# Moving two weight splits between engines and one step earlier, and two small TensorE steps one place later, in a fused attention and expert kernel

## The chip, the core and the metric

The kernel runs on one core of one Trainium2 chip. The metric is the device time of one execution in microseconds (us). PE is the matrix engine, PEld its weight loads, DVE the vector engine, ACT the scalar engine, POOL the GpSimd engine, SP the engine that issues most of the transfers (DMAs).

## The reference

The first half is attention with a window. For each of 4 batches and 8 heads, 768 rows of 64 numbers attend to the 31 rows around them and to 24 summaries, one for each block of 32 rows (the maximum of the keys, the mean of the values):

```python
scores_l = scale * np.matmul(q, k.transpose(0, 1, 3, 2))
scores_s = scale * np.einsum('bhsd,bhnd->bhsn', q, k_sum) + np.log(block)
a = softmax(concat(where(mask_l, scores_l, -1e9), scores_s))
out = a @ concat(v, v_sum)
```

The second half takes the 4 x 768 rows of 512 numbers (x), computes 8 gate logits and one more logit for each row, and picks one of 8 experts: the row's own best one where it is the first of its batch or its extra logit is negative, and otherwise the expert of the row before it. The row goes through that expert (`relu(x @ w1[e]) @ w2[e]`) and is scaled by the softmax weight of the expert.

## The kernel before

**Attention.** There are 16 pairs of heads (4 batches of 4 pairs), and each pair is done in two steps of 384 rows: 32 steps, G = 0 to 31, in `attention()`. Step G issues, in this order: the scores of step G (`s_mm`, L264 and L270), the transposes of the probabilities of step G-2 (`t_stage`, L291, copied by ACT in L292), the row maximum on DVE (L277) and six exponentials on ACT (L281) of step G, then the product with the values of step G-3 (`a_mm`, L302) and its division on DVE (`a_norm`, L313 to L315). Even steps prepare keys for a later pair on POOL (`windows`, L228), take a maximum over keys on DVE (L202) and fold the values on POOL (L213); odd steps write the summaries of keys (L231) and of values (`spread_v`, L242) on POOL. All engines work through their instructions in the order of issue. The scores of an even step G = 2n read the keys that L228 and L231 wrote for pair n.

Two score buffers alternate. From G = 32 on there are no more scores: the memory of the score buffers is given to other uses (`free_banks`), and the first `a_mm` after it writes into what was the buffer of step 31.

**The gate, beside attention.** Each of the 24 tiles of 128 rows goes through `x_tile`: (1) four transposes (L477) and a copy by ACT (L486); (2) products with the gate weights, in four quarters (L495); (3) a copy by ACT (L498); (4) a product that sums the four quarters (L506); (5) a copy by DVE to `l_all` (L508). For the first three batches the five parts are hung on steps of attention (`XT`, and the list in L1173). For the last batch they stand in `last()`, which runs 16 times `next(first)`, one eighth of a matmul stage of the first pair of expert blocks (six matmuls of 128 x 256), and after each does the parts of the gate tiles that are due: tile u starts at k = `XA[u]`, and its five parts come at k - `XA[u]` in `XL`. From G = 32 on each gate tile uses two of a pool of three PSUM banks, one for its transposes and one for parts 2 to 5.

**The routing** of a batch (`route`) is a chain of some 30 tiny DVE instructions and four PE steps (L539, L545, L551, L572), which follow one another. Such chains are generators that yield the kind of the next step ("DVE", "PE", "LONG", ...). During attention `small(n)` is called three times in each step G (with 3, 2 and 4 credits, the first after the exponentials are issued, the second before `a_norm`, the third at the end): it issues up to n steps of the first two chains in the list, a "PE" step only if two calls have passed since the chain's last step and a "PE late" step only if three have (`ON_PE`, L57). From G = 32 on `flow()` does the same by modelled times. The chain of batch 0 starts in G = 15 and picks the expert whose weights are fetched first (`have_e0`), that of batch 1 in G = 23; after it follow the index lists for the first blocks (`early`, `index`, whose L778 releases two gathers on POOL, L1001) and the gate's softmax (`gate_p`: a DVE subtraction L682, an exponential on ACT L683, and DVE sums from L687 on).

**The first expert's weights.** The fp32 weights are used as two parts, a rounded high part and a low part. Eight chunks of 128 x 1024 (j = 0 to 3 of `w1`, 4 to 7 of `w2`) are fetched by SP at the steps G in `WFETCH`; chunk j is split at step `WSPLIT[j]` for j < 4 (and at k in `WLAST` for j = 4 to 7). `split` casts on ACT (L987), then subtracts, on DVE as one instruction (L990) or on POOL as four (L995), as `WBY[j]` says ("V" or "G"). The splits stand at the end of a step, after `a_norm`.

**The experts.** Then follow pairs of blocks of 128 gathered rows (`pair`): 4 x 4 parts of six matmuls each for the first product (L1056 to L1058), relu on ACT (L1062), low part on DVE (L1064), and 16 parts for the second (L1029 to L1031). `tx` transposes gathered rows (L1012) and splits them (L1005 on ACT, L1007 on DVE).

Of the kernel before, what the change touches and what calls it, by code (L numbers as in the profile page):

```python
# [38 lines left out]
WARM = 44  # L39

WFETCH = (21, 21, 22, 22, 26, 27, 31, 32)
WSPLIT = (24, 25, 30, 31)
WBY = "VGGVVGVG"

WLAST = (2, 5, 8, 11)
XT = (0, 0, 1, 2, 2, 3)

START = ((33, 1), (34, 0), (34, 1))
XA = (0, 2, 4, 6, 8, 10)
XL = (0, 2, 3, 4, 5)  # L50

SPLIT_BY = ("VGVV", "VGVG")

# [10 lines left out]
class Kernel:  # L64
# [446 lines left out]
    def route(self, b):  # L511
# [28 lines left out]
        pm = wk.tile([NU, P], F32, name="pm")  # L540
        yield "DVE"
        v.tensor_tensor_scan(out=pm, data0=m[0:NU, 0:P], data1=self.zero[0:NU, 0:P], initial=0.0, op0=ALU.max, op1=ALU.max)
        yield "PE"
        m = self.bank("t")
        nc.tensor.transpose(out=m[:, 0:NU], in_=pm, identity=self.ident[0:NU, 0:NU])  # L545
        vm = wk.tile([P, NU], F32, name="vm")
# [569 lines left out]
    def run(self):  # L1116
# [5 lines left out]
        def at(G, point, f, *args):  # L1122
            jobs.setdefault((G, point), []).append((f, args))

        def tiles(f, b, k):
            if (b, k) not in st:
                st[b, k] = f(b, k)
            next(st[b, k], None)
# [6 lines left out]
        def wsplit(j):  # L1135
            w, q = divmod(j, NCH)
            self.split(w, q * CH, (q + 1) * CH, st.pop(("w", j)), nc.vector if WBY[j] == "V" else nc.gpsimd)

        def have_e0():
            st["e0"] = nc.values_load(self.e0[0:1, 0:1], engines=(ENG.SP,), min_val=0, max_val=E - 1)  # L1140
            for j in range(2 * NCH):
                if j < NCH:
                    at(WSPLIT[j], 1, wsplit, j)
                at(WFETCH[j], 1, wfetch, j)
# [44 lines left out]
        def last():  # L1189
            for k in range(XA[-1] + XL[-1] + 1):  # L1190
                next(first)
                if k in WLAST:
                    wsplit(NCH + WLAST.index(k))
                for u in range(NU):
                    if k - XA[u] in XL:
                        tiles(self.x_tile, B - 1, u)
                self.flow(C_T)
            self.later(self.wait(), self.route(B - 1), self.finish())
# [186 lines left out]
```

## Time and profile before

| what | value |
|---|---|
| three runs | 473.49, 472.39, 473.93 us; median 473.49 |
| the profiled execution | 473.66 us, of which the span of instructions is 471.8 |
| PE busy | 440.5 us, 93% of the span |
| DVE, ACT, POOL busy | 254.9, 216.5, 225.2 us |
| mean granted clock of PE | 0.976 |
| attention, first to last score product | to about 122.6 us |
| first matmul of the first pair of blocks | 133.80 us |

A row of the timeline reads: start, duration (of all merged instructions), engine, line, operation, what it writes <- what it reads, sizes, count, and in brackets how long its engine stood idle before it and what ended that. A row of the waits reads: who waited on whom, total us, how often, the longest. A row of the windows reads: the stretch and its length, then for PE, PEld, DVE, ACT and POOL the busy time and in parentheses the instructions begun, then the granted PE clock, the busy share of the DMA engines and GB/s.

### The profile page before, as it was taken

The page shows a single profiled execution, that of the slowest core. Times are in us where ns is not written, and L with a number is a line of the kernel's source. Part 1 is how long each engine was busy: PE and PEld are TensorE (multiplying, and loading weights), DVE is VectorE, ACT ScalarE, POOL GpSimd, SP SyncE. Part 2 cuts the span into 40 slices and gives each one's busy share as a digit, 9 for nine tenths or more (in the row PEclk, how much of TensorE's full clock was granted, in tenths as well). Part 3 has the DMA queues.
Part 4 walks back from the last instruction along what each step waited for, and adds up shares of the span by engine and source line. Part 5 has one row for each costly group of instructions (what it writes and reads, how often), then busy time and mean ns, then how long its engine had stood idle before and what let it go on. Part 6 is the DMA issues. An engine that isn't in the chain of part 4 may idle for free. (4 is left out here: it accounts for less than half of the span.)

```text
span 471.8 us, 12078 instructions
## 1 busy us (share of the span) xinstructions
PE 440.5 (93%) x4400; PEld 383.6 (81%) x4400; DVE 254.9 (54%) x603; ACT 216.5 (46%) x480; POOL 225.2 (48%) x316
## 2 busy tenths in 40 slices
PE   7799989979799999999999999999999999999990
PEld 6687767767687789798989898989779898978970
DVE  4776697868764788981222222363654227274510
ACT  4888887778745124612202020263673027266410
POOL 2686676675502421932030303094987207588820
PEclk9999999979999999999999999999999999999996
DMA  8999879988250390472020202047489403938840
GB/s 316 374 384 384 345 254 393 377 299 303 83 188 2 106 383 13 160 277 69 24 68 24 67 24 69 22 158 291 146 304 338 154 23 102 345 115 319 302 172 26
DMA packets 23623, 92.05 MB, mean 195 GB/s; under 512 B 2927, under 2 KB 3567, under 8 KB 19440
## 3 DMA queue, kind: packets, MB, share of 16 engines
q1 hardware_dynamic: 18752, 76.11, 43.6%
q0 software_dynamic: 4640, 14.68, 9.4%
q8 instruction: 41, 0.67, 0.6%
q14 instruction: 46, 0.38, 0.3%
q10 hardware_dynamic: 144, 0.20, 0.1%
HBM read 78.40 MB, written 13.11 MB: 194 GB/s over the span
## 5 line engine op out<-in xcount | busy, mean ns | idle before, releaser
L1058 PE MATMUL bs<-xT,l 128*128 128x256 f32 x384 | 108.9, 284 | 1.4 <-DVE l L990 1.4
L1056 PE MATMUL bs<-xT,h 128*128 128x256 f32 x384 | 109.9, 286 | 0.0
L1057 PE MATMUL bs<-xT,h 128*128 128x256 f32 x384 | 108.8, 283 | 0.5 <-DVE xT L1007 0.5
L1001 POOL DMA_INDIRECT xg<-x_dram,gidx x32 | 37.1, 1160 | 122.2 <-PE bt L1012 53.2
L1062 ACT ACTIVATE hT<-bs 128x512 fp32r<-128x512 f32 x48 | 28.7, 598 | 121.9 <-PE bs L1058 121.4
L1064 DVE SCALAR_TENSOR_TENSOR hT<-bs,hT 128x512 fp32r<-128x512 f32 x48 | 33.1, 690 | 90.6 <-ACT hT L1062 79.7
L1029 PE MATMUL ba<-h,hT 128*128 128x512 f32 x192 | 77.8, 405 | 0.5
L995 POOL TENSOR_TENSOR l<-stg,h 128x256 fp32r<-128x256 f32 x84 | 74.6, 921 | 2.5 <-ACT h L987 1.6
L1058 PEld LDWEIGHTS bs<-xT,l 128*128 128x128 f32 x384 | 73.5, 191 | 2.0 <-DVE l L990 2.0
L1031 PE MATMUL ba<-h,hT 128*128 128x512 f32 x192 | 75.1, 391 | 0.0
L1030 PE MATMUL ba<-l,hT 128*128 128x512 f32 x192 | 75.1, 391 | 0.0
L1057 PEld LDWEIGHTS bs<-xT,h 128*128 128x128 f32 x384 | 73.5, 192 | 1.4 <-DVE xT L1007 1.0
L1056 PEld LDWEIGHTS bs<-xT,h 128*128 128x128 f32 x384 | 73.5, 191 | 0.7 <-issue 0.2
L987 ACT CAST h<-stg 128x1024 fp32r<-128x1024 f32 x56 | 57.3, 1052 | 12.2 <-PE ba L1031 10.9
L281 ACT ACTIVATE pr<-bs,nm 128x120 f32<-128x120 f32 x192 | 51.6, 367 | 13.0 <-DVE nm L277 12.8
L990 DVE TENSOR_TENSOR l<-stg,h 128x1024 fp32r<-128x1024 f32 x35 | 47.4, 1364 | 16.3 <-ACT h L987 13.1
L1042 POOL DMA_INDIRECT out_dram<-yo,sidx x26 | 28.0, 1076 | 46.4 <-DVE yo L1041 21.3
L1029 PEld LDWEIGHTS ba<-h,hT 128*128 128x128 f32 x192 | 36.1, 188 | 8.1 <-ACT h L987 0.5
L1031 PEld LDWEIGHTS ba<-h,hT 128*128 128x128 f32 x192 | 36.0, 188 | 7.9
L1030 PEld LDWEIGHTS ba<-l,hT 128*128 128x128 f32 x192 | 36.2, 189 | 6.2
L242 POOL COPY vw<-vs 24x384 f32<-24x384 f32 x64 | 30.7, 521 | 8.7 <-ACT vs L237 6.1
L302 PE MATMUL ba<-vw,pt 120*64 120x65 f32 x768 | 31.5, 235 | 2.9 <-POOL vw L242 2.4
(236 smaller groups left out, 663.4 us busy)
## 6 DMA issues: line engine op xcount, KB each, us to landing
stg<-in_w SPq DMA_DIRECT2D x32, 1024.0 KB, 6.9
vw<-in_vW SPq DMA_DIRECT2D x16, 780.0 KB, 7.6
kp<-in_kT SPq DMA_DIRECT2D x16, 384.0 KB, 6.9
q<-in_qT SPq DMA_DIRECT2D x16, 384.0 KB, 7.4
vt<-in_vT SPq DMA_DIRECT2D x16, 384.0 KB, 8.1
x_dram<-xs SPq DMA_DIRECT2D x8, 768.0 KB, 5.1
wst<-in_w SPq DMA_DIRECT2D x8, 512.0 KB, 6.7
xg<-x_dram,gidx POOLq DMA_INDIRECT x32, 3.9
```

Source lines behind the costliest of these rows:

```text
L281: nc.scalar.activation(out=pr[:, h, u, :], in_=sp[:, h, u, :], func=AF.Exp, bias=nm[:, h, u:u + 1], scale=1.0)
L987: self.nc.scalar.copy(out=hi, in_=src)
L990: eng.tensor_tensor(out=lo, in0=src, in1=hi.bitcast(F32), op=ALU.subtract)
L995: eng.tensor_tensor(out=lo[:, p], in0=src[:, p], in1=hi[:, p].bitcast(F32), op=ALU.subtract)
L1001: self.nc.gpsimd.indirect_dma_start(out=t, out_offset=None, in_=rows, in_offset=bass.IndirectOffsetOnAxis(ap=self.gidx[:, i:i + 1], axis=0))
L1029: nc.tensor.matmul(out=ps, lhsT=ah, rhs=wh, start=first, stop=False)
L1030: nc.tensor.matmul(out=ps, lhsT=ah, rhs=wl, start=False, stop=False)
L1031: nc.tensor.matmul(out=ps, lhsT=al, rhs=wh, start=False, stop=last)
L1056: nc.tensor.matmul(out=ps[:, j], lhsT=wh, rhs=xh, start=(k == 0), stop=False)
L1057: nc.tensor.matmul(out=ps[:, j], lhsT=wh, rhs=xl, start=False, stop=False)
L1058: nc.tensor.matmul(out=ps[:, j], lhsT=wl, rhs=xh, start=False, stop=(k == KT - 1))
L1064: nc.vector.scalar_tensor_tensor(out=l, in0=ps, scalar=0.0, in1=h.bitcast(F32), op0=ALU.max, op1=ALU.subtract)
```

## The change

Four edits:

1. Chunk 0 is split in G = 23 in place of G = 24, on POOL in place of DVE.
2. Chunk 2 (G = 30) is split on DVE in place of POOL, chunk 3 (G = 31) on POOL in place of DVE.
3. In `last()` parts 4 and 5 of each gate tile come one k later, so the loop takes 17 turns in place of 16.
4. The second PE step of the routing (L545) waits for three calls of `small` in place of two, for batches 0 and 1.

```diff
 WFETCH = (21, 21, 22, 22, 26, 27, 31, 32)
-WSPLIT = (24, 25, 30, 31)
-WBY = "VGGVVGVG"
+WSPLIT = (23, 25, 30, 31)
+WBY = "GGVGVGVG"
...
-XL = (0, 2, 3, 4, 5)
+XL = (0, 2, 3, 5, 6)
...
         v.tensor_tensor_scan(out=pm, data0=m[0:NU, 0:P], data1=self.zero[0:NU, 0:P], initial=0.0, op0=ALU.max, op1=ALU.max)
-        yield "PE"
+        yield "PE late" if b < 2 else "PE"
         m = self.bank("t")
         nc.tensor.transpose(out=m[:, 0:NU], in_=pm, identity=self.ident[0:NU, 0:NU])
```

## The prediction

> **What bounds the kernel now.** I read the page first, then PE's waits, then the windows around PE's long gaps, then the timelines of each engine there.
>
> ```profile
> span 471.8 us, 12078 instructions
> ...
> PE   7799989979799999999999999999999999999990
> ```
>
> PE is the bound, and after slice 14 (11.8 us each) it is full until the last one. So what PE loses or gains before about 160 us reaches the end undiminished, and the change lies there.
>
> ```profile
> 65.46 0.19 PE L545 MATMUL bt<-ident,pm 6*128 6x6 f32 x1 [0.96 <-DVE pm L542]
> 98.20 0.24 PE L545 MATMUL bt<-ident,pm 6*128 6x6 f32 x1 [3.13 <-DVE pm L542]
> 127.90 1.48 PE L302 MATMUL ba<-vw,pt 120*64 120x65 f32 x24 [2.38 <-POOL vw L242]
> 134.72 0.39 PE L1057 MATMUL bs<-xT,h 128*128 128x256 f32 x1 [0.54 <-DVE xT L1007]
> 144.50 0.39 PE L506 MATMUL bt<-c,l 128*128 128x9 f32 x2 [0.42 <-ACT l L498]
> 153.69 0.39 PE L506 MATMUL bt<-c,l 128*128 128x9 f32 x2 [0.90 <-ACT l L498]
> ```
>
> These waits of PE between 60 and 160 us are what the edits touch: 0.96 and 3.13 (edit 4, the second with edit 1), 2.38 (edit 2), 0.42 and 0.90 (edit 3). Two of them cost more than their length:
>
> ```profile
> 93.90:97.32 3.42, 0.97 (x25) 0.81 (x24) 2.61 (x3) 2.39 (x6) 2.42 (x4) 1.00 1.05 422
> 97.40:100.70 3.30, 2.50 (x33) 2.14 (x34) 1.99 (x7) 2.76 (x8) 1.02 (x3) 0.50 0.40 155
> 100.80:104.10 3.30, 3.30 (x35) 3.15 (x34) 1.64 (x5) 2.47 (x8) 3.30 (x6) 0.50 1.00 304
> 124.63:128.04 3.41, 1.03 (x10) 0.65 (x12) 3.27 (x12) 2.53 (x9) 3.34 (x6) 1.00 0.00 0
> 128.10:131.40 3.30, 3.30 (x42) 2.84 (x41) 2.68 (x9) 2.35 (x5) 1.11 (x3) 0.50 0.58 176
> ```
>
> Where PE was busy 0.97 or 1.03 us of 3.4, the next 3.4 us ran at a granted clock of 0.50, and after a stretch with 2.50 of 3.30 one more did. A half-speed stretch that sets the end costs half of 3.4, 1.7 us. I call it a cold window. [...]
>
> **A. Edit 4, batch 0.** L545 moves from the last call of G = 17 to the first of G = 18, behind the next scores and transposes. Its input is ready then, so the 0.96 goes: between -1.0 and 0 (if DVE or ACT holds PE back by as much a step later). I take -0.9: the wait's own row is the nearest. Each later step of the chain also moves one call, `have_e0` from the end of G = 20 to the start of G = 21, still ahead of the fetches there, so SP's order stays.
>
> **B. Edits 1 and 4, batch 1 (G = 23 to 26).**
>
> ```profile
> 94.45 1.08 ACT L987 CAST h<-wst 128x1024 fp32r<-128x1024 f32 x1
> 95.56 1.35 DVE L990 TENSOR_TENSOR l<-wst,h 128x1024 fp32r<-128x1024 f32 x1 [0.81 <-ACT h L987]
> 96.83 0.90 DVE L277 TENSOR_REDUCE nm<-bs 128x6 f32<-128x720 f32 x1
> 92.98 1.62 ACT L281 ACTIVATE pr<-bs,nm 128x120 f32<-128x120 f32 x6 [1.17 <-DVE nm L277]
> 90.66 1.46 POOL L228 TENSOR_SCALAR kb<-kp 128x384 f32<-128x384 f32 x3
> 92.08 1.15 POOL L213 TENSOR_TENSOR vf<-vt 128x192 f32<-128x192 f32 x2
> 94.84 0.43 POOL L231 TENSOR_SCALAR kb<-ks 128x288 f32<-128x288 f32 x1 [1.61 <-DVE ks L202]
> 100.45 2.77 POOL L995 TENSOR_TENSOR l<-wst,h 128x256 fp32r<-128x256 f32 x4 [2.28 <-issue]
> 98.67 1.41 PE L270 MATMUL bs<-kb,q 64*64 64x120 f32 x24
> ```
>
> The 3.13 us come from DVE, which waits 0.81 for the cast of chunk 0, splits it (1.35), and only then reaches L277 and the scan. Both leave DVE. The cast fits into the 1.17 that ACT idles one step earlier. But POOL now does 2.77 us between the summaries of pair 11 and the keys of pair 13. POOL was free at 90.66; the cast ends at about 91.6 there, the split at 91.7 + 2.8 = 94.5, L228 at 96.0, L213 at 97.1, L231 at 97.6. The scores of G = 26 read what L231 writes, so PE, which would be there at 95.1, waits until 97.7; they began at 98.67 before, behind L545 and the mask products. So POOL takes DVE's place as the releaser, and the start moves by -0.8 (0 to -1.0). The gap of 2.5 us still leaves a window with about 1 us of work, so one cold window stays; the second, which followed 2.50 of 3.30 busy, may go: up to -1.7, and -2.9 (half of the 2.50 + 3.30 done cold) if both go; 0 if neither. PE is not alone in setting the pace there, so I take -1.0. B: -1.8.
>
> **C. Edit 2 and the shifted chain (G = 30 to 34).**
>
> ```profile
> 118.95 0.15 DVE L774 COPY tl<-bt 128x2 f32<-128x2 f32 x1
> 120.89 0.90 DVE L277 TENSOR_REDUCE nm<-bs 128x6 f32<-128x720 f32 x1
> 123.30 1.08 ACT L987 CAST h<-wst 128x1024 fp32r<-128x1024 f32 x1
> 124.59 0.25 DVE L687 TENSOR_REDUCE sm<-ex 128x12 f32<-128x96 f32 x1 [1.03 <-ACT ex L683]
> 126.19 1.62 ACT L281 ACTIVATE pr<-bs,nm 128x120 f32<-128x120 f32 x6 [0.88 <-DVE nm L277]
> 128.77 1.52 DVE L990 TENSOR_TENSOR l<-wst,h 128x1024 fp32r<-128x1024 f32 x1 [0.55 <-ACT h L987]
> 133.39 1.28 DVE L1007 TENSOR_TENSOR xT<-bt,xT 128x512 fp32r<-128x512 f32 x2
> ```
>
> The wait at 127.90 is booked to POOL's L242, but that copy belongs to pair 15 and the product is of pair 14. It writes into the score buffer of step 31, whose last exponential ends at 126.19 + 1.62 = 127.81, and PE starts 0.09 later. So freeing POOL does not help it, and a DVE split ahead of L277 of step 31 hurts it. From then on DVE runs nearly without a pause up to L1007, which releases PE's L1057. So I count DVE from L277 of step 30 (120.89) to the end of L1007 (134.67), 13.8 us with pauses of 1.03 and 0.55. After the change: L774 to L778 fall behind that L277, +0.6; the split is done beside an idle POOL, -0.2; DVE waits for the cast of chunk 2 (after its division at 123.4 until 124.4), 1.0; and L683 is now issued behind the exponentials of step 31, so that DVE waits from the end of L682 to the end of L281 plus one ACTIVATE, 1.65. Pauses 2.65 against 1.58: +1.1. The scores of step 30 come 0.4 earlier, as L732 moves behind them. Sum: 0.6 - 0.2 + 1.1 - 0.4 = +1.1, and +0.1 for small DVE work beside POOL's split: +1.2 (from -0.5, if DVE catches up in the time that its missing split leaves, to +2).
>
> **D. Edit 3, and three banks.**
>
> ```profile
> 142.00 0.66 PE L477 MATMUL bt<-ident,xs 128*128 128x128 f32 x4
> 142.41 0.36 PE L1056 MATMUL bs<-xT,h 128*128 128x256 f32 x1
> 148.22 0.66 PE L477 MATMUL bt<-ident,xs 128*128 128x128 f32 x4
> 142.75 0.59 ACT L486 COPY hs<-bt 128x512 f32<-128x512 f32 x1 [1.52 <-PE bt L477]
> 148.56 1.23 DVE L990 TENSOR_TENSOR l<-wst,h 128x1024 fp32r<-128x1024 f32 x1
> 149.70 0.16 DVE L508 COPY l_all<-bt 128x9 f32<-128x9 f32 x1
> ```
>
> L506 one k later finds its copy done: -0.42 - 0.90 = -1.3. But a tile now keeps its bank until k + 6 in place of k + 5, and the next tiles start every second k, so at each even k two tiles hold banks and everything else shares the third. Two places: at k = 8 the transposes of tile 4 (148.22) need the bank that L508 of tile 1 frees, and L508 stands behind the DVE split of chunk 6, so at 149.86: +1.6. At k = 4 the routing's L551 (one step later, since the DVE work modelled before it grew) needs the bank that L486 frees at 142.75 + 0.59 = 143.34, and PE would go on at 142.41: +0.9. Sum +1.2 (-1.3 if another bank is free in both, +1.6 if more waits follow). The last batch's routing starts one k later; it runs under matmuls: 0, and 0.7 at most, the length of a k.
>
> **E. Cold windows.** PE's gaps in C and D grow: it waits some 3 us for step 31, then some 2 for L1007, and 1.6 in D. Of 3.4 us that is the share of the rows above that were followed by clock 0.50, and behind L1057 PE alone sets the pace. I take one cold window more: +1.7 (0 to +3.4).
>
> **Sum**: -0.9 - 1.8 + 1.2 + 1.2 + 1.7 = +1.4 on the profiled execution's 473.66 (span 471.8 and 1.9 around it), 475.1; the median of the runs is 0.17 lower, so **475.0**.
>
> **Rivals.**
> 1. *No cold window added* (E 0): -0.3, 473.2, no change. For it: the windows run free of the gaps, and a gap cut in two by a window's end leaves both busy enough. Against: there are three such gaps.
> 2. *Faster, since the clock stays up*: a gap of 2.5 us in place of 3.13 in B triggers nothing, nor do C's and D's. B is then -0.8 - 2.9; with A, C and D, -2.2: 471.3. It decides if a window with about 1.4 us or more of work keeps the clock; the rows show 0.97 and 1.03 that did not, and none between. [...]
> 3. *The banks do not bind* (D -1.3): with the other terms -1.1, 472.4, and without E 470.7. Against it: three banks in the code.
> 4. *Clearly slower*: POOL's split of chunk 3 now lies beside DVE's chain in C. The same pair of DVE instructions beside POOL's L995 and with POOL free of it:
>
> ```profile
> 154.32 1.41 DVE L728 TENSOR_TENSOR ebt<-c,ein 128x36 bf16<-128x36 f32 x2
> 161.76 0.32 DVE L728 TENSOR_TENSOR ebt<-c,ein 128x36 bf16<-128x36 f32 x2
> ```
>
> That is 0.55 for each DVE instruction that meets one of the four pieces, +2.2 if all four meet one and nothing else gives way: 477.2. Against it: only some of DVE's instructions there are of such a kind. [...]
>
> **How the numbers follow.** About 0.3%, 1.4 us, is what a measurement here can tell from no change: faster is below 472.1, slower above 474.9. The forecast of 475.0 has 0.40, and since it lies at that line and its bounds run from 473.3 to 476.7, some 0.31 of it is slower and 0.09 the same. Rival 1 has 0.20 (0.15 the same, 0.05 faster), rival 2 has 0.17 (faster), rival 3 has 0.08 (faster 0.06, the same 0.02), rival 4 has 0.15 (slower). That makes faster 0.28, the same 0.26, slower 0.46. Both signs hold much, so the range reaches from the price of rival 2 to just above that of rival 4: 471.0 to 477.4; what is left out is the far part of rival 3 and more than one further cold window.
>
> **What would show it.** A: no idle before the first L545. B: the scores of G = 26 wait some 2.5 us, their releaser is POOL's L231, and L995 stands before the keys of pair 13; one stretch at clock 0.50 follows, not two. C: PE's wait ahead of the first product after the scores is longer than 2.38 and ends with L281, L687 waits some 1.6 for L683, and the wait for L1007 grows from 0.54 to about 2. D: no waits at L506, but one at L551 of about 0.9 and one at the transposes of the fifth gate tile of about 1.6, released by L508 behind L990. E: one more stretch at 0.50 after 130 us. The forecast is wrong if PE's waits between 60 and 160 us shrink in sum, if the bank waits are absent, or if no stretch behind the start of the first pair runs at 0.50.

## The result, and the profile after

The changed kernel takes 477.78 us (median; 477.00 to 479.78), the kernel before, run beside it, 473.57. The ratio is 1.0104 (95% interval 1.0076 to 1.0131): 4.9 us slower, where 1.4 was forecast. The direction of the forecast was right; the time lies just outside its range. The profiled execution of the changed kernel took 478.13, with a span 4.5 us longer than before. Its page, first the span, then PE's busy tenths:

```profile
span 476.3 us, 12082 instructions
...
PE   7789999989697999999999999999999999999990
```

PE is still full behind slice 14, so what was lost up to then stays lost. The rows of PE's timeline with its longest waits between 60 and 210 us (in brackets the wait and what ended it):

```profile
97.26 0.43 PE L270 MATMUL bs<-kb,q 64*64 64x120 f32 x8 [2.46 <-POOL kb L231]
126.87 1.57 PE L302 MATMUL ba<-vw,pt 120*64 120x65 f32 x24 [3.73 <-ACT pr L281]
135.17 0.38 PE L1057 MATMUL bs<-xT,h 128*128 128x256 f32 x1 [0.95 <-DVE xT L1007]
143.48 0.28 PE L551 MATMUL bt<-vm,c 128*128 128x6 f32 x1 [0.73 <-ACT hs L486]
149.00 0.43 PE L495 MATMUL bt<-hs,wg 128*32 128x128 f32 x8 [0.48 <-DVE cnt L581]
151.12 0.44 PE L477 MATMUL bt<-ident,xs 128*128 128x128 f32 x2 [1.70 <-DVE l_all L508]
203.44 0.31 PE L952 MATMUL bt<-ident,w 128*1 128x42 f32 x4 [1.65 <-DVE tot L946]
```

All the waits of the forecast are there, with the releasers it named: L231 for the scores of G = 26, L281 of step 31, L1007 (0.95 us, where about 2 was named), L486 at L551, L508 at the fifth tile's transposes. Two rows were not forecast: the 0.48 at L495, and the last one, the "words" product of `finish()`, which stood 10 us earlier in the kernel before, without a wait:

```profile
193.40 0.31 PE L952 MATMUL bt<-ident,w 128*1 128x42 f32 x4
```

Windows of the clock (columns as before; the grid is that on which the granted clock changes in this execution):

```profile
95.12:98.54 3.42, 1.28 (x29) 1.12 (x30) 1.57 (x5) 2.59 (x8) 3.36 (x8) 1.00 0.91 367
98.54:101.95 3.41, 3.41 (x34) 2.93 (x33) 1.84 (x6) 2.60 (x9) 3.33 (x7) 0.50 0.82 242
122.43:125.84 3.41, 0.71 (x6) 0.46 (x5) 2.82 (x8) 0.98 (x4) 2.52 (x5) 1.00 0.80 246
125.84:129.26 3.42, 2.39 (x28) 2.30 (x29) 2.21 (x9) 2.80 (x8) 1.24 (x2) 0.50 0.11 40
129.26:132.67 3.41, 3.41 (x34) 2.95 (x33) 3.22 (x16) 1.09 (x3) 1.56 (x3) 0.50 0.28 68
149.74:153.15 3.41, 2.03 (x18) 2.03 (x18) 1.95 (x6) 0.75 (x2) 0.00 (x0) 1.00 0.01 2
200.94:204.35 3.41, 1.76 (x17) 1.51 (x16) 3.31 (x13) 0.05 (x1) 3.41 (x6) 1.00 0.15 56
204.35:207.76 3.41, 3.41 (x18) 3.41 (x17) 3.38 (x4) 0.60 (x1) 3.24 (x3) 0.50 0.46 113
```

Four cold windows after 90 us (98.54, 125.84, 129.26, 204.35) against three before. The last follows the wait at L952.

How far PE is behind (+) or ahead (-) of the kernel before, read at its products in both traces, set against the terms of the forecast:

| stretch | forecast | measured |
|---|---|---|
| up to the scores of step 31 (121.63 before, 119.50 after): A, B | -2.7 | -2.13 |
| from there to the first L1057 (134.72, 135.17): C | +1.2 | +2.58 |
| to the first L1029 (156.04, 158.06): D | +1.2 | +1.57 |
| to the fourth pair's first product (222.33, 226.25): F, "the routing one k later" | 0 | +1.90 |
| one cold window more: E | +1.7 | in the row of F |
| from there to the end of the span | 0 | +0.58 |
| sum | +1.4 | +4.50 |

Of the last 0.58, 0.21 lie behind PE's last product; the rest was not followed up.

### The profile page after: what moved, and what is told of

The parts are those of the page before. It is cut to its first block, busy times and chain, and to the rows that moved or that the text cites. A ratio compares the mean times of both kernels' runs of the same rounds, so it can differ in the third digit from the quotient of the medians.

```text
span 476.3 us, 12082 instructions
## 1 busy us (share of the span) xinstructions
PE 440.9 (93%) x4400; PEld 383.9 (81%) x4400; DVE 258.1 (54%) x602; ACT 216.3 (45%) x480; POOL 227.9 (48%) x320
## 5 line engine op out<-in xcount | busy, mean ns | idle before, releaser
L1057 PE MATMUL bs<-xT,h 128*128 128x256 f32 x384 | 109.4, 285 | 0.9 <-DVE xT L1007 0.9
L1001 POOL DMA_INDIRECT xg<-x_dram,gidx x32 | 38.2, 1194 | 113.0 <-POOLq L1232 54.9
L995 POOL TENSOR_TENSOR l<-stg,h 128x256 fp32r<-128x256 f32 x84 | 73.5, 907 | 16.2 <-ACT h L987 15.5
L1029 PE MATMUL ba<-h,hT 128*128 128x512 f32 x192 | 77.3, 403 | 0.5 <-PEq L1242 0.2
L1057 PEld LDWEIGHTS bs<-xT,h 128*128 128x128 f32 x384 | 74.2, 193 | 1.5 <-DVE xT L1007 1.1
L1031 PE MATMUL ba<-h,hT 128*128 128x512 f32 x192 | 75.1, 391 | 0.0
L281 ACT ACTIVATE pr<-bs,nm 128x120 f32<-128x120 f32 x192 | 51.6, 367 | 12.9 <-DVE nm L277 12.4
L1029 PEld LDWEIGHTS ba<-h,hT 128*128 128x128 f32 x192 | 36.1, 188 | 7.9 <-issue 0.5
L1031 PEld LDWEIGHTS ba<-h,hT 128*128 128x128 f32 x192 | 36.0, 188 | 7.8
L302 PE MATMUL ba<-vw,pt 120*64 120x65 f32 x768 | 31.4, 234 | 4.0 <-ACT pr L281 3.7
```

The source lines that it names most:

```text
L281: nc.scalar.activation(out=pr[:, h, u, :], in_=sp[:, h, u, :], func=AF.Exp, bias=nm[:, h, u:u + 1], scale=1.0)
L995: eng.tensor_tensor(out=lo[:, p], in0=src[:, p], in1=hi[:, p].bitcast(F32), op=ALU.subtract)
L1001: self.nc.gpsimd.indirect_dma_start(out=t, out_offset=None, in_=rows, in_offset=bass.IndirectOffsetOnAxis(ap=self.gidx[:, i:i + 1], axis=0))
L1029: nc.tensor.matmul(out=ps, lhsT=ah, rhs=wh, start=first, stop=False)
L1031: nc.tensor.matmul(out=ps, lhsT=al, rhs=wh, start=False, stop=last)
L1057: nc.tensor.matmul(out=ps[:, j], lhsT=wh, rhs=xl, start=False, stop=False)
```

## Experiments

There were eighteen runs, numbered in the order in which they were made; "the fifth run" in an expectation is run 5. Ratios are to the kernel before on the same chip. In the diffs `fill(m, n)` issues n matmuls of zeros into columns m that nobody reads.

### The turn that edit 3 adds: runs 1 and 3

Run 1:

```diff
-            for k in range(XA[-1] + XL[-1] + 1):
+            for k in range(XA[-1] + XL[-1] + 2):
```

> The kernel before with one change: the loop of last() takes 17 turns in place of 16; the gate tiles keep their places, the 17th turn holds only matmuls. Theory 'order of chains': in the turn that is added the chain of batch 2 puts one more chain (the weights of the early blocks, L761) into the list, so the last batch's routing, which waits until at most one chain is left, starts some 11 us later (L539 from 160.8 to some 172 us), the words product L952 falls into the first product of the third pair at about 201 us behind DVE work that lies beside POOL's L995, PE waits there for more than 1 us and a stretch at clock 0.50 follows: 2.0 to 2.8 us more than before, 475.6 to 476.4. Step F as predicted (the routing one k later lies under matmuls): 473.6, at most 474.3, and no wait at L952. Theory 'ripple' (the wait at L952 of the changed kernel comes from the 2 us by which its first pair is late, not from the turn): 473.6.

Ratio 1.0034 (1.0009 to 1.0059), some 1.6 us slower. PE's timeline (L761: weights of the early blocks; L539: start of the last batch's routing) and the window of the wait:

```profile
165.70 0.61 PE L761 MATMUL bt<-ebp,A 128*128 128x6 bf16 x18
170.55 0.27 PE L539 MATMUL bt<-ident,val 128*6 128x128 f32 x1
201.76 0.31 PE L952 MATMUL bt<-ident,w 128*1 128x42 f32 x4 [1.65 <-DVE tot L946]
```

```profile
198.48:201.89 3.41, 1.76 (x18) 1.59 (x16) 3.31 (x11) 0.60 (x1) 3.41 (x6) 1.00 0.30 77
201.89:205.30 3.41, 3.41 (x31) 3.33 (x29) 3.38 (x6) 0.60 (x1) 3.25 (x4) 1.00 0.26 43
```

In the kernel before the order was the other one:

```profile
160.82 0.27 PE L539 MATMUL bt<-ident,val 128*6 128x128 f32 x1
173.05 0.61 PE L761 MATMUL bt<-ebp,A 128*128 128x6 bf16 x18
```

One empty turn moves L539 by 9.7 us and brings the same 1.65 at L952 as in the changed kernel. The reason stands in the code: `later()` starts the chain at once, and `wait()` at its head lets it pass only while at most one other chain is in the list. At the end of turn 16 there is one. In turn 17 batch 2's chain adds another by `also(early_p(2, 3, 1, 2))`, and the routing waits until both are done. In this execution no stretch at 0.50 followed. PE's products behind L761 in the second pair are 0.19 later than before, and the first product of the fourth pair 0.76 later, so 0.57 was lost between them: the 1.65 came, but a wait of 0.71 that the kernel before has at L887 (for DVE's L883, at 200.30) went.

Run 3, the changed kernel with the old order:

```diff
+            rest = self.steps[1:]
+            del self.steps[1:]
             self.later(self.wait(), self.route(B - 1), self.finish())
+            self.steps += rest
```

> The changed kernel with the last batch's chain put into the list ahead of the chain that batch 2 has added, so that it starts at once, as in the kernel before; the four edits and the 17 turns stay. Theory 'order of chains': the 1.65 us at L952 and the cold stretch behind it go, 2.4 to 3.0 us less than the changed kernel, 474.8 to 475.4. Theory 'one k is the price' (the later start itself, by any order): 477.8. Theory 'ripple': 477.8.

476.25 us, ratio 1.0060 (1.0034 to 1.0087). L539 is at 166.86, ahead of L761 (176.66, 179.35), there is no wait at L952, and from the products behind L761 in the second pair to the fourth pair only 0.3 is lost, in place of 2.0 in the changed kernel. So the order is the cause of the wait at L952, not the k. The time fell by less than expected, and the interval overlaps that of the changed kernel. The profiled execution was the slowest of the eight (478.92) and had cold windows elsewhere:

```profile
130.69:134.10 3.41, 1.71 (x30) 1.27 (x28) 3.20 (x15) 1.07 (x2) 0.00 (x0) 1.00 0.55 177
134.10:137.51 3.41, 3.32 (x15) 3.26 (x16) 1.26 (x5) 0.00 (x0) 0.00 (x0) 0.50 1.00 378
147.75:151.17 3.42, 1.72 (x22) 1.28 (x20) 2.34 (x7) 1.81 (x4) 0.03 (x1) 1.00 0.00 0
151.17:154.58 3.41, 2.93 (x14) 2.94 (x15) 0.84 (x6) 0.75 (x2) 0.00 (x0) 0.50 0.03 7
```

### The gate tiles and the three banks: runs 2 and 8

Run 2, edit 3 with the turn kept out:

```diff
-XL = (0, 2, 3, 4, 5)
+XL = (0, 2, 3, 5, 6)
...
-            for k in range(XA[-1] + XL[-1] + 1):
+            for k in range(XA[-1] + XL[-1]):
...
-                    if k - XA[u] in XL:
+                    if k - XA[u] in (XL if u < NU - 1 else (0, 2, 3, 4, 5)):
```

> The kernel before with edit 3 alone, but the last gate tile keeps its old places, so that the loop keeps its 16 turns and the routing its start. Step D as predicted (the three banks bind): PE's 0.42 and 0.90 at L506 go, waits of some 0.7 to 0.9 at L551 and of 1.6 to 1.7 at the transposes L477 come, in sum 1.0 to 1.6 us more than before, 474.6 to 475.2. Rival 'banks do not bind': 1.3 less, 472.3. Theory 'order of chains': no wait at L952, the words product stays at some 193 us plus the shift. Theory 'ripple': a wait at L952 and a cold stretch come here too, 2.7 more, some 477.8.

Ratio 1.0025 (1.0008 to 1.0041), some 1.2 us slower. The 0.42 and 0.90 at L506 are gone. In their place stand 0.48 at L495 and

```profile
149.44 0.44 PE L477 MATMUL bt<-ident,xs 128*128 128x128 f32 x2 [1.34 <-DVE l_all L508]
```

but nothing at L551. In the sum of the waits that is +0.5, and the first L1029 came 0.47 later than before.

Run 8, the same with the DVE split ahead of L508 taken away:

```diff
-WBY = "VGGVVGVG"
+WBY = "VGGVVGGG"
```

> The gate edit with 16 turns of the second run, and chunk 6 split on POOL in place of DVE, so that L508 of the second tile has no DVE split ahead of it. Three banks as predicted in D: the wait of 1.34 at the transposes L477 goes (under 0.3 left) and the waits at L506 stay away, so the first second-product starts some 1.2 us earlier than in that run, 473.0 (0.5 to 1.3 less than it). Rival 'L477 waits for something else': the wait stays at 1.3, 474.1.

```profile
147.37 0.33 PE L477 MATMUL bt<-ident,xs 128*128 128x128 f32 x1 [0.57 <-DVE l_all L508]
...
200.26 0.37 PE L952 MATMUL bt<-ident,w 128*1 128x42 f32 x3 [3.40 <-DVE tot L946]
```

The wait at L477 fell to 0.57, so it is the bank that L508 frees behind the split. The kernel became slower all the same, 1.0066 (1.0040 to 1.0092): `flow()` no longer counts the DVE split, batch 2's chain is one step further when `later()` is called, L761 (163.28) comes ahead of L539 (168.86) again, and L952 waits 3.40. From the products behind L761 in the second pair to the fourth pair this costs 3.5 us. A cold window (199.80 to 203.21) lies in this, too. It is the mechanism of run 1, reached without touching the loop.

### The splits and the later L545: runs 4, 6, 7 and 14

Run 4 is the changed kernel with `XL` as before.

> Edits 1, 2 and 4 without edit 3. By what the trace of the changed kernel shows: A 0.65 less, B 1.6 less, C with one cold stretch more 2.6 more, in sum 0.3 more than before, 473.9 (473.3 to 474.5), no waits at L477 and L952. By the terms of the prediction A, B and C: 1.5 less, 472.1, and 473.8 if the cold stretch of E falls into C. If the splits by themselves make the kernel slow: above 475.

Ratio 1.0011 (0.9992 to 1.0030). The first L1057 comes at 134.94 (before 134.72). L551 waits 0.73 for L486 here too, without edit 3.

Run 6, edits 1 and 4:

```diff
-WSPLIT = (24, 25, 30, 31)
-WBY = "VGGVVGVG"
+WSPLIT = (23, 25, 30, 31)
+WBY = "GGGVVGVG"
...
-        yield "PE"
+        yield "PE late" if b < 2 else "PE"
```

> Edits 1 and 4 alone: chunk 0 split in G = 23 on POOL, L545 a call later; chunks 2 and 3 stay as before, no change of the gate. A and B as the changed kernel's trace has them (0.65 and 1.6 less): 471.1 (470.4 to 472.0), the scores of G = 26 behind L231, the first pair some 2 us earlier than before. By the prediction's A and B: 2.7 less, 470.6. Rival 'the gain is lost anyway' (the end of attention is set by ACT and DVE, and the wait for L281 of step 31 grows by what B gained): 473.3, the wait ahead of the first L302 above 4.

Ratio 1.0000 (0.9983 to 1.0017): nothing gained. PE's wait for L1007, then the windows:

```profile
132.70 0.39 PE L1057 MATMUL bs<-xT,h 128*128 128x256 f32 x1 [2.63 <-DVE xT L1007]
```

```profile
130.49:133.90 3.41, 1.20 (x10) 1.18 (x11) 3.10 (x10) 0.00 (x0) 0.00 (x0) 1.00 0.44 169
133.90:137.31 3.41, 3.41 (x28) 3.35 (x27) 0.58 (x3) 1.53 (x2) 0.00 (x0) 0.50 0.82 297
```

The first pair starts 4.1 us earlier than before, then waits 2.63 for L1007, so 2.0 is left at L1057. A cold window (half of 3.41 us is 1.7) and the wait of 0.73 at L551 take that: the first L1029 is at 156.16, before at 156.04. Neither of my two theories had this: the gain is not lost at L281, it is lost behind L1057.

Run 7, edit 2 alone (`WBY = "VGVGVGVG"`):

> Edit 2 alone: chunk 2 on DVE in G = 30, chunk 3 on POOL in G = 31. If C comes from the DVE split ahead of L277 of step 31: the wait ahead of the first L302 is longer than 2.38 and the first pair starts 0.5 to 1.5 later, 474.3 to 475.9 with a cold stretch. If C comes from the chain that edits 1 and 4 shift (L683 behind the exponentials of step 31): 473.3, the first pair as before, within 0.3.

Ratio 1.0035 (1.0013 to 1.0057), 474.49 us. The first pair starts 0.64 later, L1057 0.55 later, though the scores of step 31 came 0.72 earlier. The wait ahead of the first L302 is 2.17, where more than 2.38 was expected, but 1.11 of waiting for ACT's L292 stand just ahead of it. So the split ahead of L277 of step 31 costs by itself. With edits 1 and 4 there it costs more: L1057 is at 132.70 in run 6 and at 134.94 in run 4.

Run 14, edit 4 alone:

> Edit 4 alone. Step A as predicted: the 0.96 ahead of the first L545 goes, the steps of the chain behind it move by a call, the wait of 3.13 in G = 25 stays (its DVE split is ahead of it), and the end gains nothing that can be measured, since the chain of DVE up to L1007 sets the first pair: 473.3 (472.6 to 473.9). If the later chain (L551 of batch 2 a step later beside the gate tiles) costs its 0.73: 474.0, with a wait at L551.

Ratio 1.0032 (1.0015 to 1.0048). The 0.96 ahead of L545 went. The 3.13 of batch 1 was expected to stay and went, too: 2.38 at L235 (for DVE's L206) came in its place, and no cold window followed there. PE came to the first pair 3.7 us earlier; then it waited 2.63 for L1007, two cold windows followed (130.83 to 137.66), and L551 waits 0.73 for L486.

So the wait at L551 belongs to edit 4, not to the banks of edit 3.

### The clock: runs 10, 9, 5, 12 and 11

Run 10 is the changed kernel once more.

> The changed kernel once more, beside the others. 477.8 (477.0 to 478.6). The grid of 3.41 us on which the clock is decided starts somewhere else in each execution: the waits of PE are the same as in its first profile within 0.2 us, while the stretches at 0.50 lie elsewhere or number one more or one fewer. If the grid is tied to the program: the same stretches at the same places as in the first profile (98.5, 125.8 to 132.7, 204.4).

477.49 us, ratio 1.0074 (1.0048 to 1.0100). The waits are those of the first profile (2.43 at L270, 0.73, 0.47, 1.70, and 1.65 at L952; 2.77 in place of 3.73 at L302), but the grid lies elsewhere:

```profile
149.37:152.79 3.42, 1.72 (x18) 1.65 (x15) 1.73 (x7) 0.75 (x2) 0.00 (x0) 1.00 0.01 2
152.79:156.20 3.41, 3.41 (x23) 2.80 (x22) 0.92 (x2) 0.60 (x2) 0.00 (x0) 0.50 0.02 5
203.98:207.39 3.41, 2.42 (x22) 2.37 (x23) 3.27 (x11) 0.44 (x1) 3.41 (x5) 1.00 0.00 0
```

Here the 1.70 at L477 falls into one window and brings a cold one, and the 1.65 at L952 is cut in two and brings none; in the first profile it was the other way round. At the fourth pair the executions are 3.9 and 4.0 us behind the kernel before. By the stretches of the table above, run 10 has -2.10, +2.57, +3.06, +0.45 and +0.01: the third of them holds the cold window that the fourth held in the first profile.

Run 9, the changed kernel with zeros in its waits (ahead of L270 of G = 26, of the first product of G = 32, of the first L1057, of the fifth tile's transposes and of L952, in this order):

```diff
+                if G == 26:
+                    self.fill(self.tp[:, 384:512], 27)
...
+                    if G == last_g:
+                        self.fb = self.bank("s")
+                        self.fill(self.fb[:, 0:128], 40)
...
+                    if not (i or f or j or k):
+                        self.fill(self.fb[:, 0:128], 15)
...
+        if (b, u) == (B - 1, 4):
+            self.fill(self.ps["a2"].tile([P, 512], F32, name="ba2")[:, 0:128], 18)
...
+        self.fill(m[:, 256:384], 18)
```

> The changed kernel with matmuls on zeros (128x128, some 0.05 us each) added inside five of PE's waits: 27 behind the mask products of G = 26, 40 ahead of the first product with the values in G = 32 (into a bank that is free by then, unlike in the fifth run), 15 ahead of the first L1057, 18 ahead of the transposes of the fifth gate tile, 18 ahead of L952. They are shorter than the waits, so the waits end where they did. If the cold stretches (E, and the one behind L952 in F) are what the change costs beside its waits: no stretch at 0.50 after 90 us or one at most, and 3 to 5 us less than the changed kernel beside it, 473 to 475. If the waits alone make it slow: 477 to 478, no matter what the clock does.

476.34 us, ratio 1.0059 (1.0038 to 1.0081). One cold window is left after 90 us (125.35 to 128.76), since the 40 in G = 32 themselves waited 2.73 for their bank. At the fourth pair PE is 2.8 behind the kernel before, in place of 3.9 and 4.0, although the late zeros of G = 32 made the stretch from the scores of step 31 to the first L1057 1.2 longer (16.90 in place of 15.67). So 1.1 us or more of what the change costs goes with the clock. The time lies between the two expectations, and its interval overlaps those of the changed kernel.

Runs 5 and 12 put zeros into two and three waits of the kernel before (40 ahead of L545 of batch 1, 27 ahead of the first product of G = 32, in run 12 also 10 ahead of L1057):

> The kernel before, with matmuls on zeros added in two of PE's waits: 40 of 128x128 ahead of L545 of batch 1 (some 2.1 us inside the wait of 3.13) and 27 ahead of the first product with the values in G = 32 (some 1.4 us inside the wait of 2.38). They write into columns that nobody reads; nothing else waits for them. Theory 'half a window': the clock goes to 0.50 for 3.41 us after each window of 3.41 us, cut by a grid that the program doesn't set, in which PE is busy for less than about 1.75 us; so the stretches at 97 to 104 and at 128 us go, the waits end where they did, and the time falls by 1.7 for the stretch ahead of the first pair and by 0 to 2.9 for those at 97 to 104: 468.7 to 471.6. Rival 'cold stretches cost nothing there, since DVE and ACT set the pace': no stretch at 0.50 and 473.3. Rival 'only full idleness counts' (or fill work doesn't count): stretches and time as before, 473.3.

> The kernel before with 40 matmuls on zeros ahead of L545 of batch 1, 27 ahead of the first product with the values in G = 32, now into a free bank, and 10 ahead of the first L1057. In the fifth run the first of these fills took both stretches at 97 to 104 us away and the scores of G = 27 came 2.5 us earlier against the work around them; its second fill waited for ACT and spoiled the rest. If those stretches set the end: 1.5 to 3 us less than before, 470.5 to 472. If the chain of DVE up to L1007 sets it, whatever the clock is before: 473.4, with the wait ahead of L1057 grown to 2 or more.

Both became slower: 1.0105 (1.0074 to 1.0137) and 1.0042 (1.0025 to 1.0059). The cold windows at 97 to 104 went in both, and the scores of G = 27 came 2.5 us earlier against those of G = 25. But the 27 products waited 3.77 and 2.08 us for their bank and ran behind the wait, not in it. Run 12's first L1029 came 0.18 earlier than before, its span ended 2.4 later.

Run 11, edits 1 and 4 with zeros (27 in G = 26, 20 in G = 32, 30 ahead of L1057):

> Edits 1 and 4 alone as in the sixth run, with 27 matmuls on zeros behind the mask products of G = 26, 20 ahead of the first product with the values in G = 32 and 30 ahead of the first L1057. If cold stretches eat what A and B gain: none at 0.50 between 90 and 160 us, L1057 some 2 us earlier than before and this kept (less the 0.73 at L551): 471.5 to 472.5, faster than the kernel before. If the gain is lost by work that waits for something else: 473.4.

Ratio 1.0027 (1.0010 to 1.0044): slower, though the first L1029 came 1.45 earlier than before and PE's last product 0.46 earlier.

### Behind the last product: runs 13, 15 and 16

Run 13 has 8 fp32 products of the identity matrix, in place of zeros, in G = 26 and 10 ahead of L1057, run 15 has 6 and 9, both with edits 1 and 4 (the "third pair" of the first expectation is the pair that is called the fourth here); run 16 is the kernel before with 18 short ones ahead of L545.

> Edits 1 and 4 alone, with 8 fp32 products of 128x128 (some 0.16 us each) behind the mask products of G = 26 and 10 ahead of the first L1057, that is 18 added instructions of PE in place of the 77 of the eleventh run, whose PE was 1.1 us ahead of the kernel before at the third pair but whose last signal of PE came 1.3 us after its last product, in place of 0.04. Theory 'the number of added instructions moves where PE's queue has to load code': the last signal comes right behind the last product again, the gain stays: 472.0 to 472.6, faster than before. Theory 'edits 1 and 4 gain nothing': 473.3 or more, the first second-product no earlier than 156.0.

> As the thirteenth run, with 6 and 9 added products in place of 8 and 10, so 6 instructions of PE fewer (each product has a weight load). In the thirteenth run PE's products ended 1.2 us earlier than in the kernel before, but the span was 0.6 longer, since PE's last signal came some 1.7 us after its last product; one block of instructions more was loaded (42 in place of 41). Theory 'a block of instructions that ends just before the last signal': with fewer instructions the signal follows the last product at once, the gain of 1.2 stays, 472.0 to 472.6, and no stretch at 0.50 between 90 and 160 us. Rival 'any added instruction costs that, wherever': 473.0 again.

> The kernel before with 18 short matmuls on zeros (some 1 us) inside the wait of 3.13 ahead of L545 of batch 1: as many added instructions as in the thirteenth run, no edit of the change. Theory 'block of instructions': the last signal of PE comes more than 1 us after its last product, the span behind the last product grows from 11.4 to some 13 us, 474.5 or so (less what a cold stretch at 97 to 104 that goes may give: 473.4 at least). Rival 'the tail of the thirteenth run had another cause': 11.4 as before, 473.3.

Ratios 0.9992 (0.9977 to 1.0007), 0.9996 (0.9978 to 1.0015) and 1.0032 (1.0008 to 1.0057). In all three PE's last product ended 1.1 to 1.3 us earlier than before. The span and the last product of run 16 (its L1037 is the L1031 of the kernel before), and then the last product of the kernel before:

```profile
core 0 of [0], span 472.3 us
...
458.70 0.39 PE L1037 MATMUL ba<-h,hT 128*128 128x512 f32 x1
```

```profile
460.02 0.39 PE L1031 MATMUL ba<-h,hT 128*128 128x512 f32 x1
```

From the end of that product to the end of the span it is 13.2 us in run 16 (472.3 - 459.09) and 11.4 before (471.8 - 460.41); in runs 13 and 15 it is 13.2 and 12.2. PE's next signal comes 1.28 us after the product in run 16, 0.04 before. An instruction queue of the profile moved one block more (42 in place of 41):

```profile
q8 instruction: 42, 0.69, 0.6%
```

It moved 42 in the seven runs that add products of PE and leave the warm-up as it was (5, 9, 11 to 13, 15 and 16), and 41 in both kernels and in runs 6, 14, 17 and 18. So added instructions, far ahead, can be paid behind the last product. That the queue brings PE's instructions, and that the price is the loading of its last blocks, is inferred. In run 16 the last three blocks of this queue start 3.2 and 2.4 us ahead of the end of the last product and 2.0 behind it, in the kernel before 8.9 and 2.9 ahead and 0.4 behind. Run 9 also moved 42 and had 11.4 there, with its last three 7.9 and 2.9 ahead and 0.6 behind. So the number of blocks is not enough; where a block ends was not tried by itself.

### Two versions that are faster than both: runs 17 and 18

Both make the warm-up 22 matmuls of 256 columns in place of 44 of 128, so that PE has no more instructions than before. Run 17 is the kernel before with zeros ahead of L545 of batch 1:

```diff
+        if b == 1:
+            self.fill(m[:, 128:384], 20)
```

> The kernel before with 20 matmuls on zeros of 128x256 (some 2.1 us) inside the wait of 3.13 ahead of L545 of batch 1, and with the 44 matmuls of the warm-up made 22 of double width, so that PE has no more instructions than before (4 fewer). In the run before this one 18 short ones took the stretch at 97 to 104 away and PE was 1.2 to 1.5 us ahead up to its last product, which was lost behind it. If instructions were the price: the span behind the last product is 11.4 again, 471.6 to 472.6, faster than before by 0.2 to 0.4%. If the gain is not real: 473.3.

471.46 us beside 473.88, ratio 0.9950 (0.9931 to 0.9969). PE's first L1029 is 1.7 earlier, and 11.4 us follow the last product.

Run 18 is edits 1 and 4 with zeros ahead of L270 of G = 26 and of the first L1057. The kernel that ran had 12 of 128 columns and 10 of 256, with the warm-up of run 17, not the numbers of the expectation:

> Edits 1 and 4 with 25 matmuls on zeros of 128x128 behind the mask products of G = 26 and 8 of 128x512 ahead of the first L1057, and 11 matmuls of fourfold width for the warm-up, so that PE has as many instructions as before. A and B reach the end once neither the clock nor the loading of instructions takes them back: no stretch at 0.50 between 95 and 102 us or behind L1057, first second-product some 1.4 us earlier than before, the span behind the last product 11.4 to 11.7, 472.0 to 472.6. If A and B bring nothing: 473.3.

470.69 us, ratio 0.9941 (0.9921 to 0.9961): 2.8 us faster. Its first L1029 is 2.5 earlier than before, and no window between 10 and 457 us is cold, though three waits of 1.2 to 1.5 us stand close together:

```profile
129.46:132.87 3.41, 1.89 (x17) 1.53 (x15) 3.12 (x10) 0.00 (x0) 0.00 (x0) 1.00 0.38 146
```

So a kernel with A and B can be faster than the kernel before, once no cold window behind L1057 takes the gain back. How much of the 2.8 us is theirs is not shown: run 17 has 2.4 without them, and the intervals of the two overlap. The wider warm-up was not run alone; up to G = 15 both runs are within 0.2 us of the kernel before.

## Why the prediction was right or wrong

**A and B: right where they stand.** POOL went as worked out (forecast: split done at 94.5, L228 at 96.0, L213 at 97.1, L231 at 97.6, scores at 97.7):

```profile
91.49 2.79 POOL L995 TENSOR_TENSOR l<-wst,h 128x256 fp32r<-128x256 f32 x4 [1.19 <-issue]
94.25 1.46 POOL L228 TENSOR_SCALAR kb<-kp 128x384 f32<-128x384 f32 x3
95.67 1.14 POOL L213 TENSOR_TENSOR vf<-vt 128x192 f32<-128x192 f32 x2
96.78 0.43 POOL L231 TENSOR_SCALAR kb<-ks 128x288 f32<-128x288 f32 x1
```

The scores came at 97.26, one cold window followed in place of two, and at step 31 PE was 2.1 ahead (forecast 2.7; A was 1.15 at G = 18, of which 0.65 was left at G = 20). The forecast gave the end of the 3.13 to both edits, but edit 4 has most of it: from G = 17 to step 31 PE gains 2.4 with edit 4 alone (run 14) and 3.9 with edits 1 and 4 (run 6), both without a cold window there, and 2.5 in the changed kernel with one. Entering such a gain into the sum at its full size was too much: behind it stood DVE, and in run 6 only 2.0 of it pass L1057 and are lost there.

**C: mechanism right, size wrong** (forecast +1.2, measured +2.6). DVE from L277 of step 30 to the end of L1007, after and then before:

```profile
118.48:135.12 16.64, 12.01 (x187) 10.28 (x184) 13.21 (x50) 9.45 (x25) 7.31 (x10) 0.79 0.34 102
```

```profile
120.89:134.67 13.78, 10.87 (x177) 9.01 (x177) 11.79 (x47) 9.38 (x25) 5.67 (x10) 0.88 0.37 123
```

It is 2.9 us longer; the forecast had 1.6. The two pauses that it named came nearly to the size (1.20 for the cast, where 1.0 was named, and 1.69 for L683, named 1.65). DVE's work grew by 1.4 in place of 0.5:

```profile
122.00 1.23 DVE L990 TENSOR_TENSOR l<-wst,h 128x1024 fp32r<-128x1024 f32 x1 [1.20 <-ACT h L987]
...
126.97 0.25 DVE L687 TENSOR_REDUCE sm<-ex 128x12 f32<-128x96 f32 x1 [1.69 <-ACT ex L683]
...
128.24 0.57 DVE L523 TENSOR_TENSOR eq<-l_all,mx 128x48 f32<-128x48 f32 x1
128.87 0.62 DVE L525 TENSOR_TENSOR eq<-eq,c 128x48 f32<-128x48 f32 x1
129.42 0.89 DVE L693 TENSOR_TENSOR ex<-ex,oh 128x96 f32<-128x96 f32 x1
```

The last three of these in the kernel before:

```profile
126.21 0.58 DVE L693 TENSOR_TENSOR ex<-ex,oh 128x96 f32<-128x96 f32 x1
130.21 0.19 DVE L523 TENSOR_TENSOR eq<-l_all,mx 128x48 f32<-128x48 f32 x1
130.44 0.21 DVE L525 TENSOR_TENSOR eq<-eq,c 128x48 f32<-128x48 f32 x1
```

After the change L523, L525 and L693 lie beside POOL's split of chunk 3 (128.02 to 130.83) and take 1.1 us more than before. That is rival 4, for which the forecast had set 0.1 into C and 2.2 aside. Half of it came: three of DVE's instructions met the split, with 0.38, 0.41 and 0.31 more. L693 lay beside POOL's split of chunk 2 (124.51 to 127.30) already in the kernel before, with 0.58; in run 7, with POOL free of a split, it takes 0.27.

The clock has no part in C. From the scores of step 31 to the first L1057 it takes 13.09 us in the kernel before and in runs 1 and 17, at mean granted clocks of 0.87, 1.00 and 1.00, and 15.65 to 15.67 with edits 1, 2 and 4 together (the changed kernel, runs 10, 4 and 3), at 0.78 to 0.89. Edit 2 alone makes it 1.27 longer (run 7), edits 1 and 4 alone 1.40 (run 6): both halves of C cost about the same.

**D: right in sum, wrong in part.** Measured +1.6 against +1.2. The wait of 1.70 behind L508 was as worked out (1.6), and L506's two waits went. The 0.48 at L495 was overlooked; it comes from edit 3 (run 2). The 0.73 at L551 came from edit 4 (runs 4, 6 and 14), not from the banks of edit 3 (run 2).

**E: one window too few.** Behind the scores of step 31 stand three cold windows in both profiles of the changed kernel and one in the kernel before: two more, where one was forecast. One of the two stands in C, where it cost nothing. The other stood behind L952 in one execution and behind L477 in the other, and made F's or D's stretch some 1.5 us longer (1.90 against 0.45, 3.06 against 1.57). So the price of E came once, and in the first profile it is most of F's 1.90.

**F is the step that failed:** "The last batch's routing starts one k later; it runs under matmuls: 0, and 0.7 at most, the length of a k." It started 11 us later (9.7 in run 1, where nothing else was changed), since the added turn lets another chain into the list first. L952 then had to come in the third pair, where `start()` draws the chain out step by step, and DVE did the steps ahead of it beside POOL's splits, which stand in the trace from 199.73 to 206.06:

```profile
199.21 0.67 DVE L923 SCALAR_TENSOR_TENSOR en<-end,c 128x16 f32<-128x16 f32 x1
199.92 0.65 DVE L925 SCALAR_TENSOR_TENSOR en<-start,c,en 128x16 f32<-128x16 f32 x1
200.50 0.77 DVE L928 TENSOR_TENSOR lve<-lv,c 128x16 f32<-128x16 f32 x1
```

These three took 0.23, 0.23 and 0.17 in the kernel before (187.44 to 188.02, where POOL's L995 begins at 187.88), which is 1.5 less; that this makes up most of the wait of 1.65 is inferred, as no run frees POOL there. Alone the turn cost 1.6 us (0.4 to 2.8), where nothing was forecast. Of this, 0.6 are the waits that run 1's trace shows. That the rest is a cold window, in those executions in which the grid doesn't cut the wait, is inferred from the two profiles of the changed kernel. With the old order put back (run 3) the changed kernel takes 476.25 us, inside the range of the forecast. I had read the chain's steps at their own place and not the condition under which it starts.

The second miss is the size of C, 1.4 us too small; A and B, which gave 0.6 less than forecast, come next.

The runs of the parts give 0.5 (edits 1, 2, 4) + 1.2 (edit 3 without its turn) + 1.6 (the turn) = 3.3, against 3.5 and 4.9 for the whole; with intervals of about one us each the remainder is not told apart from nothing.

Rival 2 held that a window with 1.4 us of work or more keeps the clock. The trace of the kernel before spoke against it already: PE was busy for 1.50 us from 18.82 to 22.23, and the clock was 0.50 behind it. Behind 90 us the clock fell after windows with 1.20, 1.28, 1.71, 1.72 and once 1.76 us of work, and stayed after 1.76 (run 1), 1.89 and 2.03: in these windows the line lies between 1.72 and 1.89 us of 3.41, not at 1.4. It isn't sharp: 1.76 stands on both sides, run 14 has a fall after 1.83, and of the windows with 1.5 in the first 25 us those of run 8 and of the changed kernel (1.49, from 6.38 to 9.79) kept the clock, while those of eleven other profiles lost it.

## What to carry to other kernels

Before a step is moved by one place, read the condition under which its chain starts, not only the work that it issues: a planner that counts chains turned one place into 9.7 us here. A gain on PE counts only up to the next thing that another engine sets; follow it to the first product that waits for somebody else, and then ask whether the longer wait there leaves PE too little work in a window of the clock (in the runs here, behind 90 us, 1.72 us or less of 3.41). Work on zeros inside a wait kept the clock where its bank was free (no cold window between 10 and 457 us in run 18; in run 9 one is left, and the zeros there had waited 2.73 us for their bank), and it made the kernel faster than the kernel before only where the number of PE's instructions did not grow (0.9950 and 0.9941, runs 17 and 18).

## What was not expected of the hardware

- The granted clock went by windows of 3.41 us: it fell at 22.23, 97.32 and 128.04 us in the kernel before, at 98.54, 125.84 and 204.35 in the changed kernel and at 98.17, 125.48 and 152.79 in run 10, in each a whole number of windows apart, and the two profiles of the changed kernel have their windows in different places. Behind 90 us the windows with 0.71 to 1.72 us of PE's work that are shown here were followed by one at 0.50, those at 1.00 with 1.89 or more were not; with 1.76 both came, and run 14 has a fall after 1.83. A wait of 1.65 to 1.7 us therefore cost itself, or some 1.5 us more, from one execution to the next (1.90 against 0.45 and 3.06 against 1.57 for its stretch in the two profiles of the changed kernel). Whether a cold window is followed by another does not go by its busy time alone: those with 2.39 (changed kernel) and 2.93 us (run 3) were, those with 2.71 (run 9) and 2.95 us (run 8) were not.
- 18 short matmuls inside a wait of PE, which end before the wait does, made the end of the span 1.8 us later against the last product (13.2 us behind it in run 16, 11.4 in the kernel before).
- L923, L925 and L928, DVE's instructions with two inputs of 16 elements, took 0.67, 0.65 and 0.77 us in the changed kernel, from 199.21 to 201.27, beside POOL's L995 (from 199.73), and 0.23, 0.23 and 0.17 in the kernel before; L931, a reduction with one input behind them (201.19), took 0.16 beside the same pieces. The number of inputs alone does not tell them apart: L703, a cast with one input, took 0.39 and 0.68 beside L995 (129.51 to 132.31) in run 7, and 0.18 ahead of it (128.51).
